# Output stage of a gated SSM and MLP mixer: other load order, five skip slots, a snapshot home of its own, and a reordered last group

## The chip, the cores and the metric

The kernel runs on one core of one Trainium2 chip. The metric is the device time of one execution in microseconds (us); the median of several executions is compared. A core has a matrix engine (TensorE, PE in the profile), a vector engine (VectorE, DVE), a scalar engine (ScalarE, ACT), GpSimd (POOL) and SyncE (SP). In this kernel SP issues most loads, ACT issues the stores of the output, and POOL issues the transfers that add to what is at their destination. PE writes its sums into eight PSUM banks of 128 x 512 fp32.

## The reference, cut to what matters

The input x has 2048 rows (time) of 1024. Two branches are computed from it and mixed with a gate per row:

```python
x = A_x
g = sigmoid((x * gate_w).sum(-1, keepdims=True))
Lam = Lambda_re + 1j * Lambda_im
dt = exp(log_dt); Lam_bar = exp(dt * Lam)
Bu = x @ (((Lam_bar - 1) / Lam)[:, None] * Bmat).T
h[t] = Lam_bar * h[t - 1] + Bu[t]                    # over 2048 steps
a = 2 * real(h @ Cmat.T) + x * Dskip
y = layernorm(x)
b = gelu(y @ w1 + b1) @ w2 + b2                      # 1024 -> 3584 -> 1024
out = g * a + (1 - g) * b
```

## The kernel before, in words

The program is a graph of tasks. Each task names its engine, a planned duration, a priority, the buffers that it reads and writes, and the function that emits the instruction. A planner (`schedule`) plays the graph through with the planned durations (`c_mm`, `c_act`, `c_dve`, `c_scan`, a model of the DMA queues) and fixes an order on each engine and queue; each engine then runs its list strictly in that order, and waits on semaphores where a task depends on another engine. So a changed duration in the planner can move instructions anywhere, though it changes no dependency. The order on PE is pinned: each product depends on the one before (`pe_last`).

The stages on PE, with the profile's times:

- Up to 130 us: transposes and B x (L825), results stored to DRAM as `scr_u`.
- 130 to 475 us: the MLP, in two halves of the hidden width and two halves of the rows: blocks "m" (x w1, gelu) and "b" (times w2). Partial sums of "b" go to DRAM (`scr_ac`) by POOL, the second half with an accumulating store (L1243). Beside it, DVE runs the recurrence (L970, L973, scans L984); the states go to DRAM as `scr_h`.
- From 475 us: the output stage "y", states times C, eight groups y0 to y7 of two row tiles of 128 each. Row tiles are used in the order 8 to 15, then 0 to 7 (`YORD`).

Every group in "m", "b" and "y" is a 2 x 2 block product done with seven products in place of eight (class `SG`, L1029 and, where a bank is begun, L1027). A product in "y" is 8 matmuls of 128 x 128 by 128 x 512. Each group has three PSUM banks: `a`, `e` and `b`. Its products: p1 fills `a`, and ACT copies `a` to `b` (`seed`, L1053); p5 fills `e`, ACT snapshots it (`s5`, L1045); p6 adds to `b`, ACT snapshots it (`su`, L1045); p2 completes `a`, p3 completes `e`, p7 adds to `b` (one result is taken there) and p4 adds to `b` (the last result). The pinned order from group to group is: p1 of the next group, p7 of the one before, p5, p6, p2, p3, then p4 of the one before. The last group ends with p7 and p4, one right behind the other.

What the output stage adds up for row tile k is, in the names of the tasks:

- `bb` (ACT, L1308): (1 - g) b2 into a summand buffer `AV` (eight of 128 x 1024 fp32).
- `acl` (POOL queue, L1310): the MLP's partial sums from `scr_ac`, added to it by the transfer.
- `yx` (SP queue, L1311): the tile of x into a skip buffer `XV`; `xd` (DVE, L1312): times Dskip, in place; `xa` (DVE, L1313): times g, added to the summand.
- `oa` (DVE, L1332) adds g times a snapshot to half of the summand, and `o` (DVE, L1334) adds g times a PSUM bank and writes 512 columns of the output tile; when both halves are there, `out` (ACT queue, L1339) stores 128 x 1024.
- `hg` (SP queue, L1298): the states of a group, 1 MB; `ys` (DVE, L1081): four sums and differences of them, weights of p5, p6, p7 and p3.

`y_load(yi)` records `hg`, `bb`, `acl`, `yx`, `xd`, `xa` of a group, `y_prep` the `ys`, `y_group` the rest. Where a load is recorded decides which earlier readers of its buffer it must wait for. `y_load` of groups 0 and 1 is recorded in the last "b" group, of 2 and 3 at the first y group, and of x + 3 in group x after p4 of group x - 1. From group 4 on, `hg` also waits for the last product recorded so far. The skip buffers: tiles 0 to 3 in order of use (row tiles 8 to 11) share `XV[0]`, the later ones alternate between two others. `XV[0]` is also the home of the snapshot `su` of even groups (`YU[0]`).

Of the kernel before, what the change touches and what calls it, by code (L numbers as in the profile page):

```python
# [45 lines left out]


def c_scan(N):
    return 0.12 + N / 480.0


class Buf:
# [367 lines left out]
def build(nc, A_x, A_Lambda_re, A_Lambda_im, A_B_re, A_B_im, A_C_re, A_C_im, A_log_dt, A_Dskip,  # L420
          B_x, B_w1, B_b1, B_w2, B_b2, gate_w, out, stats=None):
    x2 = A_x[0]
    out2 = out[0]
# [20 lines left out]
    g = Graph()  # L444
    es = ExitStack()
    with es:
# [30 lines left out]
        HT = AR.alloc(28672)  # L477
# [5 lines left out]
        SSM = AR.alloc(20480)  # L483
# [38 lines left out]
        def ssem(name, k, final=False):  # L522
            key = (name, k)
            if key not in slot_sems:
                slot_sems[key] = sem("d_%s%d" % (name, k), dram=final)
                if final:
                    final_sems.append(slot_sems[key])
            return slot_sems[key]
# [60 lines left out]
        def bcast(ap, off, name):  # L589
# [11 lines left out]
              reads=[b_ones], writes=[b_ident], name="ident")  # L601
# [167 lines left out]
        for k in range(LT):  # L769
            n = 1 << k  # L770
# [478 lines left out]
        H0 = [SSM, SSM + 8192] + [HT + 8192 * i for i in range(4)] + [SSM, SSM + 8192]  # L1249
        YR = HT + 49152  # L1250
        AV = [TABR + 4096 * i for i in range(4)] + [YR + 4096 * i for i in range(4)]
        XV = [SSM + 16384, YR + 16384, YR + 18432]
        DB = SSM + 18432
        OV = [YR + 20480 + 2048 * i for i in range(4)]
        YS = [SQ + 7168, HT + 32768]
        YU = [SSM + 16384, HT + 40960]
        CQ = {"B11": 0, "B21": 1, "B22": 2, "T1": 3, "T2": 4, "T3": 5, "T4": 6, "B12": 6}
        YORD = (4, 5, 6, 7, 0, 1, 2, 3)

# [34 lines left out]
        def y_load(yi):  # L1294

            qb = YORD[yi]
            o = AR.v(H0[yi], [(1, 2 * UE)])
            g.dma((52.0, yi), lambda e: e.dma_start(out=o.ap, in_=HS[qb]), 2 * UE * 128 * 2, ssem("hg", yi), reads=[b_hs[pg][qb] for pg in range(PG)], writes=[o], name="hg%d" % yi,  # L1298
                  extra=pe_last if yi > 3 else ())
            if yi == 0:  # L1300
                g.dma((51.0, 0), lambda e: e.dma_start(out=v_db.ap, in_=bass.AP(A_Dskip.tensor, A_Dskip.offset, [[0, 128], [1, D]])), 128 * D * 2, sem("d_dskb"), writes=[v_db], name="dskb")
            for t in range(2):
                n = 2 * yi + t
                k = 2 * qb + t
                av = AR.v(AV[n % 8], [(1, D)], F32)
                xi = 0 if n < 4 else 1 + n % 2
                xv = AR.v(XV[xi], [(1, D)])
                g.add("act", c_act(D, psum=False, ap_operands=1), (52.0, n), lambda e, av=av, k=k: e.activation(av.ap, v_b2.ap, AF.Copy, scale=C("GM1", k)),  # L1308
                      reads=[v_b2, bc("GM1")], writes=[av], name="bb%d" % k)
                g.dma((52.0, n), lambda e, av=av, k=k: e.dma_start(out=av.ap, in_=ACS[k], accum_op=ALU.add), 128 * D * 4, ssem("yac", n % 8), reads=[b_acs[k], av], writes=[av], name="acl%d" % k, q="pool").slack = 1.0  # L1310
                g.dma((52.0, n), lambda e, xv=xv, k=k: e.dma_start(out=xv.ap, in_=x2[k * 128:(k + 1) * 128, :]), 128 * D * 2, ssem("yx", xi), writes=[xv], name="yx%d" % k)  # L1311
                g.add("dve", c_tt16(D), (52.0, n), lambda e, xv=xv: e.tensor_tensor(xv.ap, xv.ap, v_db.ap, ALU.mult), reads=[xv, v_db], writes=[xv], name="xd%d" % k)  # L1312
                g.add("dve", c_dve(D), (52.0, n, 1), lambda e, xv=xv, av=av, k=k: e.scalar_tensor_tensor(av.ap, xv.ap, C("G", k), av.ap, ALU.mult, ALU.add),  # L1313
                      reads=[xv, av, bc("G")], writes=[av], name="xa%d" % k)

        def y_group(yi):
            qb = YORD[yi]
            st = {"A11": [hk(yi, 0, 0, k) for k in range(PT)], "A12": [hk(yi, 1, 0, k) for k in range(PT)], "A22": [hk(yi, 1, 1, k) for k in range(PT)]}
            for i in range(4):
                st["S%d" % (i + 1)] = [ysq(yi, i, k) for k in range(PT)]  # L1320
            mv = {nm: [cq(nm, k) for k in range(PT)] for nm in ("B11", "B21", "B22", "T1", "T2", "T3", "T4")}
            su, s5 = AR.v(YU[yi % 2], [(1, 512)], F32), AR.v(AO + 16384, [(1, 512)], F32)
            done = {}

            def fin(qd, q, bk):
                t, dh = qd // 2, qd % 2
                n, k = 2 * yi + t, 2 * qb + t
                a = AR.v(AV[n % 8] + dh * 2048, [(1, 512)], F32)
                o = AR.v(OV[n % 4] + dh * 1024, [(1, 512)])
                if dh == 1:  # L1330
                    sv = su if t == 0 else s5
                    g.add("dve", c_dve(512), (10.0, q - 2), lambda e: e.scalar_tensor_tensor(a.ap, sv.ap, C("G", k), a.ap, ALU.mult, ALU.add),  # L1332
                          reads=[sv, a, bc("G")], writes=[a], name="oa%d" % k)
                g.add("dve", c_dve(512), (10.0, q), lambda e: e.scalar_tensor_tensor(o.ap, V(PS[bk], 0, [(1, 512)]), C("G", k), a.ap, ALU.mult, ALU.add),  # L1334
                      reads=[b_ps[bk], a, bc("G")], writes=[o, b_ps[bk]], name="o%d.%d" % (k, dh))
                done[qd] = True
                if done.get(2 * t) and done.get(2 * t + 1):
                    ov = AR.v(OV[n % 4], [(1, D)])
                    g.dma((10.0, q + 2), lambda e: e.dma_start(out=out2[k * 128:(k + 1) * 128, :], in_=ov.ap), 128 * D * 2, ssem("out", n % 4, True), reads=[ov], name="out%d" % k, q="act")  # L1339
            return SG("_y%d" % yi, st, mv, fin, su, s5)  # L1340
# [42 lines left out]
        for n, it in enumerate(flat):  # L1383
            bi, x = it
            kind, Fh, c = blocks[bi]
            last_of_block = (n + 1 == len(flat)) or flat[n + 1][0] != bi
            nit = None if n + 1 == len(flat) else flat[n + 1]
            if (kind, Fh, c, x) == ("b", 1, 0, 3):
                y_load(0)
                y_load(1)  # L1390
            if (kind, x) == ("y", 0):
                for yi in range(2, 4):
                    y_load(yi)
            if cur is None:
                cur = make(it)
                cur.p1()

            if prev is not None:
                prev.p7()
            if kind == "b" and x + 1 < 4:  # L1400
                prep_s((bi, x + 1), seq[0] + 4)
            if kind == "b" and Fh == 1 and c == 0 and x == 3:
                y_prep(0, seq[0] + 4)
            if kind == "y":
                if x + 1 < 8:
                    y_prep(x + 1, seq[0] + 4)
            if not early5:
                cur.p5()
            early5 = False
            cur.p6()  # L1410
            cur.p2()
            cur.p3()
            if prev is not None:
                prev.p4()
                if kind == "y" and 1 <= x and x + 3 < 8:
                    y_load(x + 3)
                if kind == "m" and x > 0:
                    w1_next(18)
            prev, cur = cur, pend
            pend = None  # L1420
            if last_of_block:
                if nit is None:
                    prev.p7()
                    prev.p4()
                else:
                    nk = blocks[nit[0]][0]
                    if nk == "b":
                        prep = True
                        b0 = None

                        cur = make(nit)
                        prev.p7()
                        cur.p1()
                        prev.p4()
                        w1_next(20)
                        prep_s(nit, seq[0])
                        pend = make((nit[0], nit[1] + 1))
                        pend.p1()
                    else:
                        cur = make(nit)  # L1440
                        prev.p7()
                        cur.p1()
                        cur.p5()
                        early5 = True
                        prev.p4()
                    prev = None
                if (kind, Fh, c) == ("m", 1, 0):
                    ct_load(seq[0] + 20)

                if kind == "m":  # L1450
                    if (Fh, c) == (0, 0):
                        xn_load(1, seq[0] + 20)
                    elif (Fh, c) == (1, 1):
                        xn_load(0, seq[0] + 20)
                elif (Fh, c) == (0, 1):
                    w2_load(1, seq[0] + 30)
# [43 lines left out]
```

## Time and profile before

| what | us |
|---|---|
| median of 7 runs | 579.3 (577.74 to 583.58) |
| the profiled execution | 583.58 |
| its span | 581.8 |
| PE busy in the span | 558.1 |
| DVE busy in the span | 479.8 |
| output stage, from p1 of y0 to the end of the span | 474.8 to 581.8 |
| load of a skip tile, issue to landing (16 of them): shortest, median, longest | 2.6, 7.4, 11.2 |
| load of a group's states, issue to landing (8): shortest, median, longest | 6.0, 7.1, 11.5 |

The profile is of one execution, the slowest of the seven. PE's busy time is nearly the span, so the time is made where PE waits; the busy times of the other engines matter only through those waits. A wait is named after what came last, and that may itself have been held up by what stands ahead of it in its engine's or queue's list. Task names like `yx11` carry the row tile, `hg3`, `seed_y1` the group; they follow from the order of the instructions of a line on its engine.

### The profile page before, as it was taken

The numbers are of one execution on the slowest core, as the hardware profiler recorded it, in microseconds if no ns is written. First come the engines' busy times: TensorE is split into PE (matmuls) and PEld (weight loads), VectorE is DVE, ScalarE is ACT, GpSimd is POOL, SyncE is SP. The second block draws the span as 40 slices with busy tenths as digits, with TensorE's granted clock in tenths as the row PEclk, the third lists the DMA queues.
The fourth block names the chain that finished last, engine by engine and source line by source line (L and its number), as shares of the span: only waits on it lengthen the run. The fifth ranks groups of instructions, "written<-read, shape, count | busy, mean of one in ns | idle before, by whom it ended". The sixth has DMA issues, their size and how long they took to land.

```text
span 581.8 us, 7338 instructions
## 1 busy us (share of the span) xinstructions
PE 558.1 (96%) x2608; PEld 255.2 (44%) x2657; DVE 479.8 (82%) x817; ACT 271.1 (47%) x433; POOL 76.5 (13%) x110
## 2 busy tenths in 40 slices
PE   4999999997999999999999999999999999799997
PEld 3544444443444444444444444444444444344442
DVE  2799719949999999999999999999346785779843
ACT  2844871345674335864326673336863352222210
POOL 0070144000000111001120000130100231111000
PEclk9999999999999999999999999999999999999999
DMA  8999848999399733648379699987999599799601
GB/s 249 252 265 378 320 118 255 298 287 381 123 345 231 254 145 152 257 163 293 159 262 353 197 279 264 208 158 196 291 292 198 90 235 267 203 276 270 210 37 55
DMA packets 124543, 134.76 MB, mean 232 GB/s; under 512 B 70482, under 2 KB 100178, under 8 KB 123482
## 3 DMA queue, kind: packets, MB, share of 16 engines
q1 hardware_dynamic: 99664, 70.81, 43.6%
q0 software_dynamic: 11232, 46.40, 28.9%
q10 hardware_dynamic: 13610, 17.08, 8.6%
q8 instruction: 21, 0.34, 0.3%
q14 instruction: 16, 0.13, 0.1%
HBM read 63.74 MB, written 54.80 MB: 204 GB/s over the span
## 4 chain that ended last, share of the span: by engine, by line
PE 66%; DVE 16%; DMA 9%; issue 6%; ACT 1%; POOL 1%; SPq 1%; ACTq 0%; DVEq 0%; POOLq 0%
PE ps L1029 39%; PE ps L1027 14%; PE ps L825 11%; DVE ar L1081 4%; DMA ar<-scr_ac 3%; DVE ar L970 3%; DVE ar L984 3%; DMA ar<-in_A_x_dram 3%; DVE ar L973 2%; DMA ar<-in_B_w_dram 2%; DVE ar L1163 2%; DMA scr_ac<-ar 2%; DVE ar L871 1%; POOL scr_ac L1243 1%; PE ps L666 1%
## 5 line engine op out<-in xcount | busy, mean ns | idle before, releaser
L1029 PE MATMUL ps<-ar 128*128 128x512 f16 (+1 forms) x1419 | 327.1, 380 | 9.5 <-ACT ps L1053 4.0
L1029 PEld LDWEIGHTS ps<-ar 128*128 128x128 f16 (+1 forms) x1440 | 140.7, 98 | 180.6 <-ACT ps L1053 5.1
L1027 PE MATMUL ps<-ar 128*128 128x512 f16 (+1 forms) x560 | 137.5, 379 | 2.0 <-DVE ar L1081 1.2
L1081 DVE TENSOR_TENSOR ar<-ar 128x896 f16<-128x896 bf16 (+8 forms) x176 | 118.2, 707 | 18.4 <-DMA ar<-scr_xn 7.6
L825 PE MATMUL ps<-ar 128*128 128x512 bf16 x500 | 111.6, 382 | 0.9 <-issue 0.4
L984 DVE TENSOR_TENSOR_SCAN ar<-cst,init,ar 128x256 bf16<-128x256 f32 x128 | 86.9, 732 | 0.3
L1027 PEld LDWEIGHTS ps<-ar 128*128 128x128 bf16 (+1 forms) x576 | 56.1, 98 | 70.5 <-DVE ar L1081 3.1
L970 DVE TENSOR_TENSOR ar<-ar 128x2048 bf16<-128x2048 bf16 x64 | 77.0, 1217 | 2.8 <-DMA ar<-scr_u 2.8
L825 PEld LDWEIGHTS ps<-ar 128*128 128x128 bf16 x512 | 50.0, 99 | 60.6 <-issue 2.1
L832 ACT ACTIVATE ar<-ps 128x512 bf16<-128x512 f32 x64 | 37.0, 595 | 49.5 <-PE ps L825 27.9
L1045 ACT ACTIVATE ar<-ps 128x512 f32<-128x512 f32 x72 | 42.2, 592 | 36.3 <-PE ps L1027 26.3
L1053 ACT ACTIVATE ps<-ps 128x512 f32<-128x512 f32 x52 | 30.3, 582 | 40.4 <-PE ps L1027 32.6
L1159 ACT ACTIVATE ar<-ps,cst 128x512 bf16<-128x512 f32 x56 | 38.4, 685 | 20.7 <-PE ps L1029 20.1
L1163 DVE TENSOR_TENSOR ar<-ps,ar 128x512 f32<-128x512 f32 x56 | 38.0, 679 | 11.3 <-PE ps L1029 11.0
L1046 ACT ACTIVATE ar<-ps,cst 128x512 f32<-128x512 f32 x32 | 22.0, 687 | 52.9 <-PE ps L1027 33.2
L1165 ACT ACTIVATE ar<-ar,cst 128x512 bf16<-128x512 f32 x56 | 40.1, 716 | 13.0 <-DVE ar L1163 12.9
L973 DVE TENSOR_TENSOR ar<-ar 128x1024 bf16<-128x1024 bf16 x64 | 42.0, 684 | 0.3
L1231 ACT ACTIVATE ar<-ps,cst 128x512 f32<-128x512 f32 x32 | 22.0, 687 | 42.5 <-PE ps L1029 42.5
L1334 DVE SCALAR_TENSOR_TENSOR ar<-ps,cst,ar 128x512 bf16<-128x512 f32 x32 | 23.9, 748 | 12.4 <-PE ps L1029 12.4
L1308 ACT ACTIVATE ar<-ar,cst 128x1024 f32<-128x1024 bf16 x16 | 18.3, 1146 | 28.5 <-DVE ar L1334 27.1
L1234 DVE SCALAR_TENSOR_TENSOR ar<-ps,cst,ar 128x512 f32<-128x512 f32 x32 | 23.7, 740 | 7.4 <-PE ps L1029 6.6
L1310 POOL DMA_DIRECT2D ar<-scr_ac x16 | 14.0, 878 | 89.9 <-ACT ar L1308 58.3
(98 smaller groups left out, 228.0 us busy)
## 6 DMA issues: line engine op xcount, KB each, us to landing
scr_ac<-ar POOLq DMA_DIRECT2D x32, 512.0 KB, 7.0
scr_w<-ar POOLq DMA_DIRECT2D x14, 896.0 KB, 5.7
ar<-scr_w SPq DMA_DIRECT2D x14, 896.0 KB, 6.1
ar<-in_A_x_dram SPq DMA_DIRECT2D x32, 256.0 KB, 7.1
scr_u<-ar ACTq DMA_DIRECT2D x32, 256.0 KB, 5.9
ar<-scr_u SPq DMA_DIRECT2D x16, 512.0 KB, 7.7
scr_h<-ar POOLq DMA_DIRECT2D x16, 512.0 KB, 6.0
ar<-scr_ac POOLq DMA_DIRECT2D x16, 512.0 KB, 9.5
```

Of the source, the lines that this page charges most:

```text
L825: ins = e.matmul(V(PS[bk], 0, [(1, CH)]), ws[dt].ap, xs[dt].ap, start=(dt == 0), stop=(dt == DT - 1))
L832: g.add("act", c_act(CH), pr, lambda e, ev=ev, bk=bk: e.activation(ev.ap, V(PS[bk], 0, [(T, 2), (1, T)]), AF.Copy), reads=[b_ps[bk]], writ ...
L970: g.add("dve", c_tt16(UE), pri(i), lambda e: e.tensor_tensor(o.ap, a.ap, tbl.ap, ALU.mult), reads=[a, tbl], writes=[o], name=nm + tag)
L973: g.add("dve", c_tt16(UE // 2), pri(i), lambda e: e.tensor_tensor(o.ap, a.ap, b.ap, op), reads=[a, b], writes=[o], name=nm + tag)
L984: lambda e, pt=pt, ri=ri, vin=vin, go=go: e.tensor_tensor_scan(go.ap, Cb("R", pt, T), vin.ap, V(INIT, pt * 2 + ri, [(1, 1)]), ALU.mult, AL ...
L1027: ins = e.matmul(V(PS[bk], 0, [(1, n)]), st[i].ap, mv[i].ap, start=(i == 0), stop=(i == K - 1))
L1029: ins = e.matmul(V(PS[bk], 0, [(1, n)]), st[i].ap, mv[i].ap, start=False, stop=(i == K - 1), skip_group_check=True)
L1045: return e.activation(o.ap, V(PS[bk], 0, [(1, 512)]), AF.Copy)
L1081: g.add("dve", c_tt16(n), (10.0, q), lambda e: e.tensor_tensor(o.ap, a.ap, b.ap, op), reads=[a, b], writes=[o], name=nm).slack = slack
L1159: g.add("act", c_act(512, ap_operands=1), (10.0, q + 1), lambda e: e.activation(o.ap, V(PS[bk], 0, [(1, 512)]), AF.Gelu_apprx_tanh, bias=C ...
L1163: g.add("dve", c_dve(512), (10.0, q - 2), lambda e: e.tensor_tensor(sv.ap, V(PS[bk], 0, [(1, 512)]), sv.ap, ALU.add), reads=[b_ps[bk], sv] ...
L1165: g.add("act", c_act(512, psum=False, ap_operands=1), (10.0, q + 3), lambda e: e.activation(o.ap, sv.ap, AF.Gelu_apprx_tanh, bias=C("B1", ...
```

## The change

Six edits, all but the first in the output stage:

- the planned duration of a scan is longer (0.719 us in place of 0.653 for 256 columns);
- two more skip buffers, so that tiles from the fifth on go through four in place of two;
- the snapshot `su` of even groups gets memory of its own in place of `XV[0]`;
- `y_load` of group 3 is no longer recorded at the first group, and that of later groups one group later than before: two groups ahead in place of three; `hg` waits for the last recorded product from group 3 on;
- in the last group p7 comes before p3 in place of after p4 of the group before;
- the last group's output is stored in halves of 512 columns, each when it is ready.

```diff
 def c_scan(N):
-    return 0.12 + N / 480.0
+    return 0.15 + N / 450.0
...
-        XV = [SSM + 16384, YR + 16384, YR + 18432]
+        XV = [SSM + 16384, YR + 16384, YR + 18432, HT + 43008, HT + 45056]
...
-        YU = [SSM + 16384, HT + 40960]
+        YU = [HT + 47104, HT + 40960]
...
-                  extra=pe_last if yi > 3 else ())
+                  extra=pe_last if yi > 2 else ())
...
-                xi = 0 if n < 4 else 1 + n % 2
+                xi = 0 if n < 4 else 1 + n % 4
...
-                if done.get(2 * t) and done.get(2 * t + 1):
+                if yi == 7:
+                    g.dma((10.0, q + 2), lambda e: e.dma_start(out=out2[k * 128:(k + 1) * 128, dh * 512:(dh + 1) * 512], in_=o.ap), 128 * 1024, ssem("outl", qd, True), reads=[o], name="out%d.%d" % (k, dh), q="act")
+                elif done.get(2 * t) and done.get(2 * t + 1):
...
             if (kind, x) == ("y", 0):
-                for yi in range(2, 4):
-                    y_load(yi)
+                y_load(2)
...
             cur.p6()
             cur.p2()
+            if nit is None:
+                cur.p7()
             cur.p3()
             if prev is not None:
                 prev.p4()
-                if kind == "y" and 1 <= x and x + 3 < 8:
-                    y_load(x + 3)
+                if kind == "y" and 1 <= x and x + 2 < 8:
+                    y_load(x + 2)
...
                 if nit is None:
-                    prev.p7()
                     prev.p4()
```

## The prediction

> **What bounds the kernel now.** I read the page's busy line first, then what TensorE (PE) waits for, then the timeline around those waits, then the DMA queues in the same stretch.
>
> ```profile
> PE 558.1 (96%) x2608; PEld 255.2 (44%) x2657; DVE 479.8 (82%) x817; ACT 271.1 (47%) x433; POOL 76.5 (13%) x110
> ```
>
> PE is the bound: 558.1 of 581.8 us, and back-to-back matmuls of 512 columns start 216 ns apart. No matmul is added or removed, so the change can only touch PE's idle time. The waits of PE (total us, times, longest):
>
> ```profile
> PE ps L650 <- DMA ar<-in_A_x_dram: 7.7, 2, 5.8
> PE ps L1029 <- ACT ps L1053: 4.0, 1, 4.0
> PE ps L1029 <- ACT ar L1045: 3.0, 1, 3.0
> PE ps L1027 <- DVE ar L1081: 1.2, 3, 0.5
> PE ps L1029 <- DVE ar L1334: 0.9, 1, 0.9
> ```
>
> 7.7 us is the start, out of reach. 4.0 and 0.9 lie in the output stage, 3.0 in the first MLP group, 1.2 at three starts of a second-GEMM block. So about 5 us (0.9%) is the most that the edits of the output stage can win. The timeline where the output stage begins (start, length, engine, line; in brackets the idle time before and who ended it):
>
> ```profile
> 486.31 0.69 DVE L1312 TENSOR_TENSOR ar<-ar 128x1024 bf16<-128x1024 bf16 x1 [2.06 <-DMA ar<-in_A_x_dram]
> ...
> 488.31 0.74 DVE L1334 SCALAR_TENSOR_TENSOR ar<-ps,cst,ar 128x512 bf16<-128x512 f32 x1
> ...
> 489.08 0.36 ACTq L1339 DMA_DIRECT2D out_dram<-ar  x1
> 489.54 0.58 ACT L1053 ACTIVATE ps<-ps 128x512 f32<-128x512 f32 x1 [7.50 <-DVE ar L1334]
> 490.04 1.14 ACT L1308 ACTIVATE ar<-ar,cst 128x1024 f32<-128x1024 bf16 x1
> ...
> 490.18 7.08 PE L1029 MATMUL ps<-ar 128*128 128x512 f16 x32
> ...
> 500.54 0.69 DVE L1312 TENSOR_TENSOR ar<-ar 128x1024 bf16<-128x1024 bf16 x1 [2.35 <-DMA ar<-in_A_x_dram]
> ...
> 505.82 0.58 ACT L1053 ACTIVATE ps<-ps 128x512 f32<-128x512 f32 x1
> ...
> 506.45 7.08 PE L1029 MATMUL ps<-ar 128*128 128x512 f16 x32 [4.01 <-ACT ps L1053]
> ```
>
> One chain appears twice. A skip row tile (256 KB of x) lands late; DVE's `xd` (L1312) waits for it; the output sum `o` (L1334) is queued behind on DVE; ACT's store of that output waits for `o`; ACT's `seed` (L1053) is queued behind the store; PE's p6 needs the seed. It costs 0.3 us at p6 of group y1 (PE was free at 489.9, started 490.18) and 4.2 us at p6 of y2 (502.3 to 506.45). So what counts is when each skip tile lands, and what stands ahead of each seed. In this stretch two queues share the DMA engines; the DMA view of 478.4 to 485:
>
> ```profile
> q0 software_dynamic: 288, 1.05, 79.7%
> q1 hardware_dynamic: 291, 0.58, 26.2%
> ```
>
> Equal packet counts, 44 per us each. The two skip tiles loaded there (`yx12`, `yx13`) are about 144 packets each, so one takes 3.3 us while POOL's 512 KB accumulating transfers (q0) are pending.
>
> The tail: PE waits 0.91 us for DVE to empty a PSUM bank before the last product, and the last sum follows.
>
> ```profile
> 575.80 0.75 DVE L1334 SCALAR_TENSOR_TENSOR ar<-ps,cst,ar 128x512 bf16<-128x512 f32 x1 [1.04 <-PE ps L1029]
> ...
> 576.61 1.90 PE L1029 MATMUL ps<-ar 128*128 128x512 f16 x8 [0.91 <-DVE ar L1334]
> ...
> 578.55 0.75 DVE L1334 SCALAR_TENSOR_TENSOR ar<-ps,cst,ar 128x512 bf16<-128x512 f32 x1 [2.00 <-PE ps L1029]
> ```
>
> [...] after the 3.0 us wait, the 8 matmuls from 142.41 took 3.46 us instead of 1.73. After the 4.0 us wait it did not drop (506.45: 32 matmuls in 7.08 us).
>
> **The change part by part.**
>
> *Skip tiles.* Before, tiles 8 to 11 (in order of use) share one slot: each load waits for the `xa` of the tile before. `yx12` to `yx15` go through two slots, so `yx15` and `yx14` cannot be issued until `xa13` and `xa12` are done (488.42, 493.17). After, four slots serve tiles from 12 on. In the built order SP issues, behind one another, `yx14`, `yx15` (when p3 of the last second-GEMM group is done, near 471.7), `yx12`, `yx13` (474.75, as now), then `yx11`. That last one matters. In the kernel before it was issued at 449.41 and landed at 452.00, because DVE did `xd10`, `xa10` early. In the built order after, `yx10` comes behind the four C transposes and `xd10`, `xa10` stand behind `ac1.3.1` and `ys4_1`. Those two take place at 471.7 to 473.1; 0.69 + 1.28 us more put `xa10` at 475.0, and `yx11` is issued about 475.6, fifth in the queue.
> Landing: under this load the first packet of `yx15` came 3.6 us after its issue (488.42 to 492.02); so the five start near 475.3, and 5 x 144 / 44 = 16.4 us later, at 491.7, the fifth is through; semaphores came 0.5 to 1.3 us after last packets. **`yx11` lands near 492.6.** POOL's loads hold their times: they lose about 1 us to the two early tiles and win it back because `hg3` (1 MB, 479.76 to 491.22) has moved to after p4 of y0. Hence `acl12` (491.84) is not late.
>
> *First wait.* DVE after: ..., `xd12`, `xd11`, `o8.1`, .... `xd11` 492.6, `o8.1` ends 492.6 + 0.65 + 0.75 = 494.0. ACT after: store, then `bb0` (L1308), then the seed of y1, where before the seed came first. From end of `o8.1` to p6 took 1.13 us (489.05 to 490.18); `bb0` adds its pitch of 1.03. p6 of y1 starts 496.2: a wait of 6.3 us instead of 0.3. Queued behind on DVE: `xa11`, `xa12`, `o9.1` (done 497.9; p4 of y0 needs it at 501.4: no wait).
>
> *Second wait.* From 496.2, p6 of y2 is due seven products of 1.73 us later, 508.3. DVE after `o9.1` (497.9) has nine operations up to `o10.1`: `xa15` and `xa13` of 1.28 and seven of about 0.65, so 505.0. Store, `bb2`, seed as above: 507.2. So this 4.2 us wait goes, with 1 us to spare. Sum of both: 6.3 - 0.3 - 4.2 = **+1.8 us**.
>
> *Later groups.* An `hg` load is now issued one group (12.1 us) before its p1 instead of two; the median landing is 7.1 us, the longest 11.5, and the prep `ys` needs another 2.5 us but p5 comes 3.5 us after p1. I take 0; if cover is gone, up to 2 us once. `bb`, `acl` keep their POOL places. The snapshot's own home frees `su` of y0 from `xa11`: su of y0 was not waited for (481.45), so 0; without this edit it would now wait for `xa11`.
>
> *Clock.* [...] 0 to 2.5 us, I take **+0.8**.
>
> *Tail.* p7 of y7 moves ahead of p3, so two products (3.4 us) lie between it and p4: -0.9. Its `su` has p2's 1.73 us to be made in, against 0.6. Four half stores replace two stores: two more issues of 0.34 us on ACT, idle there. The last store moves 128 KB: DVE's last sum ended 579.30, the span 581.8; a 256 KB store ran its packets in 0.83 us, so -0.2 (0 to -0.4). **-1.1.**
>
> *Planner cost.* A scan was planned at 0.653 us, now at 0.719; measured 0.732. This reorders DVE from 100 us on. First MLP group: `cadd0.0.1` moves behind two more scans (2 x 0.66): the 3.0 us wait, s5 behind that gelu, grows 1.3; DVE is full there from 131 to 180, later `cadd`s are up to 1.9 late against 0.6 us of room before a seed: +0.9 (0 to 2.5). Starts of second-GEMM blocks: the first gets 0.84 us more work ahead of its `hs1`, part of that same lateness; the second and third (waits of 0.25 and 0.54) get 0.6 and 2.6 us less SSM work ahead: -0.8. **+0.1.**
>
> Sum: 1.8 + 0.8 - 1.1 + 0.1 = **+1.6 us**. The profiled execution took 583.58 (span 581.8), the median is 579.3: the profiled one is the slowest of the seven, so some of its waits may be smaller elsewhere. 583.6 would become 585.2; on the median I say **580.9**.
>
> **Rivals.** *A: `yx11` is no bottleneck, 0.22.* If skip tiles get through faster than 44 packets per us (an uncongested one landed in 2.6 us), `xd12` sets `o8.1` at 488, p6 of y1 waits 0.5, and the y2 wait goes: -4.0 - 1.1 and 0.1: 574.3; if it lands at 489, half: 577. For: the runs without profile are shorter. Against: the packet counts.
> *B: the clock decides, 0.18, slower.* [...] 2.5 us instead of 0.8, 1.8 + 2.5 - 1.1 + 0.1 = +3.3, 582.6. It decides once the clock is at half for over 4.2 us (a loss of 2.1). For: the drop after 139 us. Against: the 4.0 us wait left the clock alone.
> *C: DVE's new order costs the first MLP group its whole bound, 0.15, slower.* 2.5 instead of 0.9: 1.8 + 0.8 - 1.1 + 1.7 = +3.2, 582.5. For: DVE has no gap there from 131 to 180, and seeds have 0.6 us of room. Against: each `cadd` that is late in one group leaves less ahead of the next.
> *D: the change doesn't do what it says.* Neither wait depends on the slots, as it would be if skip tiles were held by the transfers alone; then only the tail is won, -1.1, 578.2. It lies in the main case (0.45, its own range 577.5 to 582.2).
>
> **Numbers.** Half a percent is 2.9 us, about what a measurement of this kernel can tell from no change. Faster by that needs A: 0.22. Slower needs B or C, or both (585): 0.33. The main case and D make up 0.45. The range, 575.4 to 585.0, goes from a little above A's full gain to B and C together.
>
> **What would show it.** Right: PE's wait for L1053 moves from 502 to about 490 and is near 6 us, `xd11` (L1312) waiting for a skip tile near 492; no wait before the last product; the waits of L1027 for L1081 down to one. Wrong: L1053 gone from PE's waits (A), or the granted clock at half after 496 for over 3 us (B).

## The result, and the profile after

The changed kernel takes 586.71 us (median of 15 runs, 582.65 to 591.57), the kernel before, beside it, 580.08 (36 runs). Ratio 1.0107, 95% interval 1.008 to 1.0134: **slower by 6.2 us (4.6 to 7.8)**, outside the predicted range (575.4 to 585.0). All ratios here leave out runs more than 1.5% above the fastest of their kernel; medians are over all runs, so the two can differ a little.

The profiled execution took 587.56 us, span 585.5. Busy times, then PE's waits (total us, times, longest):

```profile
PE 558.8 (95%) x2607; PEld 256.0 (44%) x2657; DVE 481.3 (82%) x817; ACT 270.7 (46%) x433; POOL 74.1 (13%) x110
```

```profile
PE ps L1029 <- ACT ps L1053: 7.0, 2, 6.8
PE ps L650 <- DMA ar<-in_A_x_dram: 6.6, 2, 5.6
PE ps L1029 <- ACT ar L1045: 5.7, 1, 5.7
PE ps L1027 <- DVE ar L1081: 1.2, 3, 0.6
```

PE's work is the same (558.8 against 558.1). The wait for L1334 is gone: the tail edit did what it says. The seed's wait (L1053) is still one long wait, 6.8 us instead of 4.0. The wait for a snapshot (L1045) in the first MLP group went from 3.0 to 5.7.

The timelines of DVE, ACT and PE where the output stage begins (start, length, engine, line; in brackets the idle time before it and who ended it):

```profile
487.36 0.69 DVE L1312 TENSOR_TENSOR ar<-ar 128x1024 bf16<-128x1024 bf16 x1
493.76 0.69 DVE L1312 TENSOR_TENSOR ar<-ar 128x1024 bf16<-128x1024 bf16 x1 [5.71 <-DMA ar<-in_A_x_dram]
494.37 0.74 DVE L1334 SCALAR_TENSOR_TENSOR ar<-ps,cst,ar 128x512 bf16<-128x512 f32 x1
```

```profile
495.15 0.36 ACTq L1341 DMA_DIRECT2D out_dram<-ar  x1
495.55 1.15 ACT L1308 ACTIVATE ar<-ar,cst 128x1024 f32<-128x1024 bf16 x1 [13.08 <-DVE ar L1334]
496.61 0.58 ACT L1053 ACTIVATE ps<-ps 128x512 f32<-128x512 f32 x1
```

```profile
497.24 9.23 PE L1029 MATMUL ps<-ar 128*128 128x512 f16 x32 [6.77 <-ACT ps L1053]
...
511.49 3.83 PE L1029 MATMUL ps<-ar 128*128 128x512 f16 x17
```

This is the predicted chain, link by link. `yx11`, issued at 476.08 as the fifth skip load, landed at 493.74; `xd11` (the second L1312) waited 5.71 us for it; `o8.1` (L1334) stood behind; then the store, `bb0` (L1308), the seed (L1053), and p6 of y1 at 497.24 after 6.77 us of idle PE. p6 of y2 (511.49) has no wait. What the prediction had too small stands in the length of the first PE row: 9.23 us for 32 matmuls that take 7.08 at full clock. The table of the windows around it (stretch, its length, busy times; the sixth value after the comma, PEclk, is the granted clock):

```profile
490.00:494.80 4.80, 0.47 (x3) 0.00 (x0) 1.04 (x2) 0.00 (x0) 0.00 (x0) 1.00 1.06 245
494.80:501.60 6.80, 4.36 (x11) 1.61 (x12) 6.80 (x9) 2.75 (x4) 0.85 (x1) 0.50 0.77 163
501.60:508.00 6.40, 6.35 (x30) 2.88 (x30) 6.30 (x9) 1.15 (x1) 0.29 (x1) 1.00 0.61 181
```

The clock is at half for 6.8 us, from 2.4 us before PE came back until 4.4 us after: 9.23 - 7.08 = 2.15 us lost.

The first MLP group of the changed kernel, on PE (here too the clock was at half for 6.8 us, from 139.8 to 146.7; 8 matmuls take 1.90 us at full clock, as in e11's row below):

```profile
143.19 3.59 PE L1029 MATMUL ps<-ar 128*128 128x512 bf16 x8 [5.70 <-ACT ar L1045]
```

And the tail, the last products of PE without a gap, then DVE's last sum:

```profile
571.92 10.52 PE L1029 MATMUL ps<-ar 128*128 128x512 f16 x47
```

```profile
582.49 0.75 DVE L1334 SCALAR_TENSOR_TENSOR ar<-ps,cst,ar 128x512 bf16<-128x512 f32 x1 [0.97 <-PE ps L1029]
```

### The profile page after: what moved, and what is told of

Same layout as the page of the kernel before. It is cut to its first block, busy times and chain, and to the rows that moved or that the text cites. A ratio compares the mean times of both kernels' runs of the same rounds, so it can differ in the third digit from the quotient of the medians.

```text
span 585.5 us, 7342 instructions
## 1 busy us (share of the span) xinstructions
PE 558.8 (95%) x2607; PEld 256.0 (44%) x2657; DVE 481.3 (82%) x817; ACT 270.7 (46%) x433; POOL 74.1 (13%) x110
## 4 chain that ended last, share of the span: by engine, by line
PE 78%; DVE 12%; DMA 6%; issue 2%; SPq 1%; ACT 1%; ACTq 0%; DVEq 0%
PE ps L1029 48%; PE ps L1027 18%; PE ps L825 11%; DMA ar<-in_A_x_dram 4%; DVE ar L984 3%; DVE ar L970 3%; DMA ar<-in_B_w_dram 2%; DVE ar L973 2%; DVE ar L1081 2%; DVE ar L871 1%; DVE ar L1163 1%; PE ps L666 1%; SPq L957 0%; PE ps L891 0%; DVE ar L1334 0%
## 5 line engine op out<-in xcount | busy, mean ns | idle before, releaser
L1027 PE MATMUL ps<-ar 128*128 128x512 f16 (+1 forms) x560 | 137.5, 379 | 1.9 <-DVE ar L1081 1.2
L1081 DVE TENSOR_TENSOR ar<-ar 128x896 f16<-128x896 bf16 (+8 forms) x176 | 117.2, 708 | 18.4 <-DMA ar<-scr_xn 5.8
L825 PE MATMUL ps<-ar 128*128 128x512 bf16 x500 | 110.6, 380 | 0.9 <-issue 0.4
L1027 PEld LDWEIGHTS ps<-ar 128*128 128x128 bf16 (+1 forms) x576 | 56.2, 98 | 70.4 <-DVE ar L1081 3.1
L825 PEld LDWEIGHTS ps<-ar 128*128 128x128 bf16 x512 | 49.9, 98 | 59.8 <-issue 1.0
L1045 ACT ACTIVATE ar<-ps 128x512 f32<-128x512 f32 x72 | 42.2, 592 | 39.7 <-PE ps L1027 27.3
L832 ACT ACTIVATE ar<-ps 128x512 bf16<-128x512 f32 x64 | 36.9, 595 | 48.8 <-PE ps L825 26.5
L1163 DVE TENSOR_TENSOR ar<-ps,ar 128x512 f32<-128x512 f32 x56 | 38.2, 682 | 14.0 <-PE ps L1029 12.1
L1053 ACT ACTIVATE ps<-ps 128x512 f32<-128x512 f32 x52 | 30.3, 583 | 36.0 <-PE ps L1027 34.8
L1308 ACT ACTIVATE ar<-ar,cst 128x1024 f32<-128x1024 bf16 x16 | 18.2, 1145 | 34.2 <-DVE ar L1334 32.4
L1334 DVE SCALAR_TENSOR_TENSOR ar<-ps,cst,ar 128x512 bf16<-128x512 f32 x32 | 23.9, 747 | 11.3 <-PE ps L1029 11.0
```

Source lines behind the costliest of these rows:

```text
L825: ins = e.matmul(V(PS[bk], 0, [(1, CH)]), ws[dt].ap, xs[dt].ap, start=(dt == 0), stop=(dt == DT - 1))
L832: g.add("act", c_act(CH), pr, lambda e, ev=ev, bk=bk: e.activation(ev.ap, V(PS[bk], 0, [(T, 2), (1, T)]), AF.Copy), reads=[b_ps[bk]], writ ...
L1027: ins = e.matmul(V(PS[bk], 0, [(1, n)]), st[i].ap, mv[i].ap, start=(i == 0), stop=(i == K - 1))
L1045: return e.activation(o.ap, V(PS[bk], 0, [(1, 512)]), AF.Copy)
L1081: g.add("dve", c_tt16(n), (10.0, q), lambda e: e.tensor_tensor(o.ap, a.ap, b.ap, op), reads=[a, b], writes=[o], name=nm).slack = slack
L1163: g.add("dve", c_dve(512), (10.0, q - 2), lambda e: e.tensor_tensor(sv.ap, V(PS[bk], 0, [(1, 512)]), sv.ap, ALU.add), reads=[b_ps[bk], sv] ...
```

## The experiments

The theory with which I began them: the buffers and the tail bring little, and the *planned scan cost* loses the time, in two places: the order around block 11 in the output stage (late `xd10`, late `yx11`, a long wait, two windows of half clock), and the order ahead of the output stage. Rivals: the output stage's order alone, the front alone, or the edits of loads and buffers themselves.

All kernels of the study, with the edit of each. "Half-clock windows" is worked out from each run's mean granted clock: (1 - clock) x span x 2 / 3.41 us, averaged over the runs. A window here is 3.41 us: the clock stood at half for 3.41 us in the trace of before and twice for 6.83 us in that of the changed kernel. One costs at most 1.7 us of matmul time, if PE is busy in all of it (in e0, 32 matmuls behind a wait took 8.76 us in place of 7.08).

| kernel | scan cost | median us (runs) | ratio to before (95%) | half-clock windows per run |
|---|---|---|---|---|
| before | old | 579.5 to 581.1 | 1 | 1.7 to 1.9 |
| changed | new | 586.71 (15) | 1.0107 (1.008 to 1.0134) | 3.1 |
| e1: scan cost alone | new | 588.43 (4) | 1.0142 (1.0089 to 1.0195) | 3.1 |
| e2: all but the scan cost | old | 579.72 (14) | 0.997 (0.9936 to 1.0005) | 1.5 |
| e3: last group alone | old | 579.63 (22) | 0.9995 (0.9971 to 1.002) | 1.6 |
| e4: changed, first skip products early | new | 587.12 (6) | 1.0105 (1.0061 to 1.015) | 2.9 |
| e5: new for units 0 to 4 | mixed | 582.97 (22) | 1.0031 (1.0007 to 1.0055) | 1.8 |
| e6: new from unit 5 on | mixed | 582.39 (22) | 1.0061 (1.004 to 1.0082) | 2.6 |
| e7: e2, blocks 12 to 15 later | old | 573.18 (6) | 0.9887 (0.9839 to 0.9935) | 0.7 |
| e8: e2, block 8's product late | old | 582.11 (14) | 1.0024 (0.9998 to 1.005) | 2.5 |
| e9: e4 and e7's edit | new | 579.69 (22) | 0.9963 (0.9937 to 0.999) | 1.2 |
| e10: new for units 5 to 11 | mixed | 578.65 (22) | 0.997 (0.9946 to 0.9994) | 1.2 |
| e11: e9, old for unit 0 | mixed | 575.48 (21) | 0.9931 (0.9905 to 0.9957) | 0.4 |
| e14: new for units 12 to 15 | mixed | 578.06 (22) | 0.9975 (0.9951 to 1.0) | 1.2 |
| e15: new for unit 0 | mixed | 585.66 (20) | 1.0063 (1.0031 to 1.0095) | 2.7 |

A unit is one SSM step of DVE, 8 scans (four channel groups, real and imaginary part); two halves of the channels by eight blocks of 256 rows make 16 units. e12 and e13 gave no time; e14 and e15 are the same two kernels. Differences between two kernels below are differences of ratios times 580 us; their half-widths are the root of the summed squares.

### The kernel before once more

> The kernel before, unchanged, for a second profile. The change moved the median by 6.6 us but the two profiled executions by only 4.0. Theory X (the first profile of before is of a slow execution): here one of its waits is smaller, the 3.0 us one before the first MLP group with its half clock, or the 4.2 us one at p6 of y2, and the span is near 578. Theory Y (the waits of before are fixed): both waits come again within 0.5 us.

One execution, 576.8 us. PE's waits:

```profile
PE ps L650 <- DMA ar<-in_A_x_dram: 5.7, 1, 5.7
PE ps L1029 <- ACT ps L1053: 4.0, 1, 4.0
PE ps L1027 <- DVE ar L1081: 1.4, 3, 0.6
PE ps L1029 <- DVE ar L1334: 0.9, 1, 0.9
```

The 3.0 us wait for L1045 isn't there. The profile from which I predicted had caught the kernel before with a wait in its first MLP group that this execution doesn't have. The waits of the output stage are the same to a tenth.

### The scan cost alone, all but it, and the tail alone

e1 is the kernel before with the first hunk of the diff. e2 is the changed kernel without it:

```diff
 def c_scan(N):
-    return 0.15 + N / 450.0
+    return 0.12 + N / 480.0
```

e3 is the kernel before with the last group's order and half stores only.

> The kernel before with nothing but the longer planned scan (0.15 + N / 450). In its built order xd10 and xa10 stand behind ac1.3.1, so yx11 is issued near 475.6, third behind yx12 and yx13, and lands near 490; su of y0 still shares the slot of that tile, so it waits for xa11 (near 494.5), and p7 of y0 (due 486.4) for it. Theory S (the planned scan cost makes the loss, by the place of xd10): PE waits about 8 us at p7 of y0, slower than before by 4 to 8 us. Theory L (the new slots and load order make the loss, the scan cost does not): within 1.5 us of before. Theory M (the loss is in the first MLP group): slower by about 1 to 3 us, with the wait of 3.0 us near 139 grown to 4 to 6 and no long wait at 486.

> The changed kernel with the old planned scan (0.12 + N / 480), all edits of the output stage kept. xd10, xa10, xd11, xa11 stand early on DVE again and yx11 is issued at 449; but o8.1 now stands behind xd12 and xd13, and yx13 is fourth of four skip tiles issued from 471.7: 4 x 144 packets at 44 per us from 475.3 end at 488.4, landing near 489.3. o8.1 ends near 491.3, seed of y1 behind out8 and bb0, p6 of y1 near 493.5: a wait of 3.6 us in place of 0.3, the wait of 4.2 us at y2 gone, 1.1 us won at the end. Theory S: -1.5 us against before, give or take 1.5, so at least 4 us faster than the changed kernel. Theory L: as slow as the changed kernel, +5 to +7. Theory M: -1 to -4.

> The kernel before with only the last group's new product order and the half stores. All theories: the wait of 0.9 us before the last product goes, and the last store is shorter; -1.1 us (-0.9 to -1.3), a ratio of 0.998. If the half stores or two more issues cost anything, nearer to -0.7.

The planned cost of a scan, which computes nothing, is the cause: alone it loses 8.2 us (1.0142), and without it the changed kernel is level with the kernel before. Where PE idles longest in the output stage: the line of e1's waits (it lies at p7 of y0, 484 to 492 us, since `su` of y0 has to wait for `xa11` in the old home of the snapshot), then PE's rows of e2 and e3:

```profile
PE ps L1029 <- ACT ar L1045: 7.4, 1, 7.4
```

```profile
493.17 8.77 PE L1029 MATMUL ps<-ar 128*128 128x512 f16 x32 [3.89 <-ACT ps L1053]
```

```profile
499.89 5.49 PE L1029 MATMUL ps<-ar 128*128 128x512 f16 x18 [4.05 <-ACT ps L1053]
```

e3 keeps the wait of the kernel before (at p6 of y2) and loses only the 0.9 before the last product; its time does not change measurably (-0.3 us, -1.7 to +1.2). In e2 the wait at y2 is gone and one of the same size stands at p6 of y1. DVE's rows of e2 say why the new buffers did not remove it:

```profile
486.50 0.69 DVE L1312 TENSOR_TENSOR ar<-ar 128x1024 bf16<-128x1024 bf16 x1 [0.50 <-DMA ar<-in_A_x_dram]
489.70 0.69 DVE L1312 TENSOR_TENSOR ar<-ar 128x1024 bf16<-128x1024 bf16 x1 [2.51 <-DMA ar<-in_A_x_dram]
490.31 0.74 DVE L1334 SCALAR_TENSOR_TENSOR ar<-ps,cst,ar 128x512 bf16<-128x512 f32 x1
```

`o8.1`, ready to go, stands behind `xd12` and `xd13`, whose tiles are four and five places further on in the output and still in the DMA queue. In the kernel before `o8.1` stood behind the same two products, but there `yx12` and `yx13` were the first two of these loads (issued from 474.75). The new buffers let `yx14` and `yx15` be issued ahead of them (from 470.97 in e2), so that `yx13` is the fourth: `xd13` begins at 489.70 in place of 486.31.

### Splitting the scan cost by place

```diff
# e4
-                g.add("dve", c_tt16(D), (52.0, n), lambda e, xv=xv: e.tensor_tensor(xv.ap, xv.ap, v_db.ap, ALU.mult), reads=[xv, v_db], writes=[xv], name="xd%d" % k)
-                g.add("dve", c_dve(D), (52.0, n, 1), lambda e, xv=xv, av=av, k=k: e.scalar_tensor_tensor(av.ap, xv.ap, C("G", k), av.ap, ALU.mult, ALU.add),
+                g.add("dve", c_tt16(D), ((9.0, n) if n < 4 else (52.0, n)), lambda e, xv=xv: e.tensor_tensor(xv.ap, xv.ap, v_db.ap, ALU.mult), reads=[xv, v_db], writes=[xv], name="xd%d" % k)
+                g.add("dve", c_dve(D), ((9.0, n, 1) if n < 4 else (52.0, n, 1)), lambda e, xv=xv, av=av, k=k: e.scalar_tensor_tensor(av.ap, xv.ap, C("G", k), av.ap, ALU.mult, ALU.add),
# e5
-                    g.add("dve", c_scan(T), pri(10 + ri * 4 + a),
+                    g.add("dve", c_scan(T) if un < 5 else 0.12 + T / 480.0, pri(10 + ri * 4 + a),
# e6
-                    g.add("dve", c_scan(T), pri(10 + ri * 4 + a),
+                    g.add("dve", 0.12 + T / 480.0 if un < 5 else c_scan(T), pri(10 + ri * 4 + a),
```

> The changed kernel with one edit: the scaled products of the first four skip blocks (xd and xa, n under 4) get priority 9.0 instead of 52.0. VectorE then does xd10, xa10, xd11, xa11 ahead of the last scan's products, as with the old scan cost, and block 11's load is issued right after block 10's; the front part is the changed kernel's own. Theory Y (half of the loss is the order around block 11, half is the front part): the 6.8 us wait on L1053 falls to about 3.9 at the first output slice, as in the all-but-scan kernel, with one window of half clock instead of two; the time is 583.3 us, 3 to 4 below the changed kernel. Theory O (the order around block 11 alone): 579.7. Theory F (the front part alone, the first MLP group's wait of 5.7 us on L1045): 586.7, no change.

> The changed kernel with the new scan cost for the first five SSM units only, the old one after that. VectorE's order is that of the changed kernel in the front part, and that of the all-but-scan kernel at the output stage. Theory Y: 583.3 us, the wait on L1045 ahead of the first MLP group at 5 to 6 us and the one on L1053 at about 3.9 us. Theory O: 579.7. Theory F: 586.7.

> The changed kernel with the old scan cost for the first five SSM units and the new one after that: VectorE's order is that of the kernel before in the front part, and that of the changed kernel at the output stage (block 11's load fifth in its queue, xd11 late, o8.1 behind it). Theory Y: 583.3 us, no wait of over 3 us ahead of the first MLP group, and 6.8 us on L1053 at the first output slice with two windows of half clock. Theory O: 586.7. Theory F: 579.7.

The medians of e5 and e6 fell where both places count (582.97 and 582.39 for 583.3). The two share out all units between them: e5 is 3.5 us (half-width 2.4) above e2 and e6 5.3 (2.3), together 8.8, and the changed kernel is 7.9 (2.5) above e2. e5 idles 3.5 us at p6 of y1, e6 7.0 us with two windows of half clock (mean clock 0.994 over 579.8 us). The wait of 5 to 6 us at L1045 that was expected of e5 is not in its trace; PE idles 3.1 us earlier there, at L825 for ACT's L832. e4's trace did what was expected in the output stage,

```profile
492.12 8.77 PE L1029 MATMUL ps<-ar 128*128 128x512 f16 x32 [4.24 <-ACT ps L1053]
```

but its time was 587.12, not 583.3: a miss that a theory of two additive places does not explain (taken up below). The trace is of the fastest of its six executions (581.67 us), so it does not show what the others lost.

### The order around block 11 by itself

e8 is e2 with one task placed later by the planner, `xd8` (n = 0 is row tile 8; `xd9` and `xd10` follow through the slot that they share), and holds the changed kernel's order from `xd9` on:

```diff
-                g.add("dve", c_tt16(D), (52.0, n), lambda e, xv=xv: e.tensor_tensor(xv.ap, xv.ap, v_db.ap, ALU.mult), reads=[xv, v_db], writes=[xv], name="xd%d" % k)
+                g.add("dve", c_tt16(D), (52.0, n), lambda e, xv=xv: e.tensor_tensor(xv.ap, xv.ap, v_db.ap, ALU.mult), reads=[xv, v_db], writes=[xv], name="xd%d" % k).slack = 8.0 if n == 0 else 0.0
```

> The all-but-scan kernel (old scan cost everywhere) with the scaled product of block 10 alone placed 8 us later in the planner's order. From block 8's product on, every queue then holds the changed kernel's order (block 11's load fifth among the skip loads, xd12, xd11 and then o8.1 on VectorE), while everything up to the third MLP block keeps the old order. If the order around block 11 costs by itself what the traces show (from the start of the wait on L1053 to the end 95.4 and 95.6 us in the changed kernel and with the old front, 92.0 and 92.4 with the early order): a wait of 6.8 us on L1053 with two windows of half clock, and 579.7 + 3.4 = 583.1 us. Rival: the whole loss sits ahead of the output stage, as the early-skip-products kernel's time of 587.1 suggests: 579.7, no change from the all-but-scan kernel.

Two rows of its trace, DVE and PE:

```profile
483.40 0.69 DVE L1312 TENSOR_TENSOR ar<-ar 128x1024 bf16<-128x1024 bf16 x1 [5.70 <-DMA ar<-in_A_x_dram]
```

```profile
486.88 8.53 PE L1029 MATMUL ps<-ar 128*128 128x512 f16 x32 [6.13 <-ACT ps L1053]
```

The long wait, the two windows (mean clock 0.994 over 574.4 us) and +3.1 us against e2 (0.6 to 5.6; expected 3.4) come with this order alone. The traces agree: from the start of y0's seed (ACT, L1053) to the end of the span it is 107.2 to 108.7 us with the late order (e8, e6, the changed kernel), and 103.1 to 105.5 where the other edits of the output stage stand with the early one (e2, e4, e5, e10, e14, e15). e4 has 105.5 there and the changed kernel 108.5: in the output stage e4's edit did bring its 3 us.

### Taking the queue in front of `o8.1` away

e7 is e2 with the same kind of edit on other tasks, `.slack = 12.0 if 4 <= n < 8 else 0.0`: the products of blocks 12 to 15 no longer stand ahead of `o8.1`.

> The all-but-scan kernel (old scan cost everywhere) with the scaled products of blocks 12 to 15 placed up to 12 us later in the planner's order, so that o8.1 on VectorE is no longer queued behind products that wait for their loads. If o8.1 behind those waits is what holds the first output slice, o8.1 ends near 486 instead of 491, the 3.9 us wait on L1053 goes or falls under 1 us, with no half clock there, and the time is about 575.5, 3 to 5 below both kernels. Rival: the wait comes back a slice later, since o9.0 is now queued behind xd12 and xa12, which wait for the load of acl12 at about 491.8: a wait of 2 to 4 us on L1053 at p6 of y2, and the time stays at 579 to 580.

DVE and PE:

```profile
485.53 0.75 DVE L1334 SCALAR_TENSOR_TENSOR ar<-ps,cst,ar 128x512 bf16<-128x512 f32 x1 [0.98 <-PE ps L1029]
```

```profile
490.51 7.07 PE L1029 MATMUL ps<-ar 128*128 128x512 f16 x32
...
502.59 2.75 PE L1029 MATMUL ps<-ar 128*128 128x512 f16 x12
```

`o8.1` now waits for PE's result only, no seed is waited for at y1 (490.51) or y2 (502.59), and the rival (the wait returns at y2) is refuted. 573.18 us, ratio 0.9887: faster than both kernels, 4.8 us below e2 (1.4 to 8.2). Up to `o8.1` the loads are issued in the order of e2 (behind `yx2`, `hg3` and `hg4` come earlier); what differs ahead of this sum is DVE's list. From the start of y0's seed to the end it is 99.4 to 99.7 us in the traces of e7, e9 and e11, in place of e2's 105.2.

### Which units lose the time ahead of the output stage

e9 has the new cost everywhere, e4's early products and e7's edit; e11 is e9 with the old cost for unit 0. e10, e14 and e15 are e2 with the new cost for a few units (in the manner of e5's line: `5 <= un < 12`, `un >= 12`, `un < 1`).

> The changed kernel with its new scan cost kept everywhere, and two edits at the output stage: the first four skip products at priority 9.0 (early), those of blocks 12 to 15 placed up to 12 us later. VectorE's order at the output stage is that of the later-skip-sums kernel, the rest is the changed kernel's. No wait of over 1 us on L1053 is expected. If the new scan cost loses 3.6 us ahead of the output stage and 3.4 there: 573.2 + 3.6 = 576.8 us. Rival, all of the 7 us lost ahead of the output stage: 580.2.

> The changed kernel with the new scan cost for SSM units 5 to 11 alone, the old one before and after; the output stage keeps the early order. If the first five units (up to about the first MLP group) carry what is lost ahead of the output stage: 579.7 us, the time of the all-but-scan kernel. Rival, the middle units carry about 4 us of it (early-skip-products 587.1 less new-front-old-order 583.0): 583.7, with waits between the first second-GEMM group and the output stage longer than before.

> The kernel with the new scan cost and no wait in the output stage (579.7 us), with the old scan cost for SSM unit 0 alone. VectorE then does nb0.0 ahead of the table scales G and GM1, for which it waits until about 81 to 84 us, instead of behind them (1.3 us of work moves into that idle time), and the sum cadd0.0.1 of the first MLP group comes behind two scans instead of four (1.3 us earlier). If these two moves carry what is lost ahead of the output stage: from the end of VectorE's wait on L932 to fx3_0.2 32.8 us instead of 34.0, no wait of over 3 us on L1045 after 135 us, and 576 us, 3.7 lower. Rival: the loss sits in the later order of the first five units, and the time stays at 579.7; if the two moves count but once, without the clock that a wait costs, 578.3.

> The all-but-scan kernel with the new scan cost for SSM units 12 to 15 alone; the output stage keeps the early order. If the first five units and the late order at block 11 carry the whole loss: 579.7 us, a ratio of 0.997 to the kernel before. Rival: the last units carry what two pairs of runs leave over (0.4 to 0.7%): 582 to 584 us.

> The all-but-scan kernel with the new scan cost for SSM unit 0 alone: nb0.0 goes behind G and GM1, and cadd0.0.1 behind five scans instead of two; the output stage keeps the early order. If unit 0's two moves carry what the first five units cost: a wait of 3 us or more on L1045 near 136 to 140 us, fx3_0.2 34 us after G instead of 32.8, and 583.2 us, a ratio of 1.003. Rival: the order of units 1 to 4 carries it: 579.7 us, a ratio of 0.997.

Against e2, the new cost for units 5 to 11 changes nothing measurable (0.0, half-width 2.4), for units 12 to 15 nothing (+0.3, 2.5); for units 0 to 4 it costs 3.5 (2.4), and for **unit 0 alone 5.4 us (2.7)**; the last two are not apart by the noise. In the other direction, e11 against e9 is -1.9 (2.2) by the ratios and -4.2 by the medians: the same sign, not clear by itself. What unit 0's cost moves first is seen on DVE, in the changed kernel and then in e11. First around 70 to 85 us:

```profile
70.22 1.22 DVE L970 TENSOR_TENSOR ar<-ar 128x2048 bf16<-128x2048 bf16 x1
82.72 0.22 DVE L934 TENSOR_SCALAR cst<-cst 128x16 f32<-128x16 f32 x1 [11.28 <-ACT cst L932]
...
83.00 1.21 DVE L970 TENSOR_TENSOR ar<-ar 128x2048 bf16<-128x2048 bf16 x1
```

```profile
70.07 1.22 DVE L970 TENSOR_TENSOR ar<-ar 128x2048 bf16<-128x2048 bf16 x1
...
71.29 1.22 DVE L970 TENSOR_TENSOR ar<-ar 128x2048 bf16<-128x2048 bf16 x1
83.71 0.20 DVE L934 TENSOR_SCALAR cst<-cst 128x16 f32<-128x16 f32 x1 [11.21 <-ACT cst L932]
```

DVE waits 11 us for the gate (L932). The second product, `nb0.0`, was done ahead of that wait and is now done after it: 1.2 us of work taken out of idle time and put behind it. Then the first sum of the MLP, `cadd0.0.1` (L1163), again the changed kernel and e11:

```profile
138.63 2.68 DVE L984 TENSOR_TENSOR_SCAN ar<-cst,init,ar 128x256 bf16<-128x256 f32 x4
141.23 0.67 DVE L1163 TENSOR_TENSOR ar<-ps,ar 128x512 f32<-128x512 f32 x1
```

```profile
136.17 1.39 DVE L984 TENSOR_TENSOR_SCAN ar<-cst,init,ar 128x256 bf16<-128x256 f32 x2
137.48 0.67 DVE L1163 TENSOR_TENSOR ar<-ps,ar 128x512 f32<-128x512 f32 x1
```

Four scans ahead of it instead of two: 1.3 us more. PE's row of e11 to be held against the changed kernel's 5.70 us at 143.19, and that of e15:

```profile
139.50 1.90 PE L1029 MATMUL ps<-ar 128*128 128x512 bf16 x8 [0.69 <-ACT ar L1045]
```

```profile
146.11 3.52 PE L1029 MATMUL ps<-ar 128*128 128x512 bf16 x8 [3.08 <-ACT ar L1045]
```

3.52 us for 8 matmuls in e15, against 1.90 in e11, is half clock again. e15's output stage takes as long as e2's (104.8 and 105.2 us from the seed of y0), so its loss lies ahead of it. The other traces point the same way. From 60 to 160 us PE waits for other engines 3.6 to 8.1 us in each of the six with the new cost for unit 0 (e1, e4, e5, e9, e15, the changed kernel); of the ten with the old one, seven wait 1.2 us at most, and three (before, e2, e7) 3.0 to 5.2. Not all of it lies in the first MLP group: e1 and e5 have no wait at L1045 there, and idle 3.3 and 3.1 us at L825 instead, as e2 and e7 do.

e15, with e11 of the same sign, shows that unit 0's planned cost by itself costs about what is lost ahead of the output stage. By which of its moves is not shown. Every kernel with the new cost for unit 0 has the two above, and they are not all: the traces of e2 and e15 have another operation (by line or shape) in 298 of the 817 places of DVE's list, from 70 to 473 us.

### What stays open

Two pairs leave more than these parts: e6 against e8 (2.1, half-width 1.9) and e4 against e5 (4.3, 2.9), in which the new cost from unit 5 on is added. e10 and e14 show nothing for those units one set at a time, so either it takes both sets, or e4 (6 runs) is off. Also open is what makes the stretch from 115 to 145 us differ so much between executions of one order: in the traces with the old cost for unit 0, DVE's waits for the normalized rows (`scr_xn`) come to 1.4 us in one and 10.1 in another. The averages above rest on many runs for that reason.

## Why the prediction was wrong, step by step

| step | predicted us | measured us |
|---|---|---|
| `yx11` lands | 492.6 | 493.74 |
| wait at p6 of y1 in place of that at y2 | +1.8 | +2.3 in the trace (6.77 - 0.3 - 4.2) |
| clock in the output stage | +0.8 (0 to 2.5) | +2.15 in the trace |
| `hg` one group ahead, the snapshot's own home | 0; without the home a wait for `xa11` | no wait of either kind in the trace; e1, without the home, waits 7.4 for `xa11` |
| tail | -1.1 | -0.9 and -0.24 in the trace; e3's time -0.3 (-1.7 to +1.2) |
| planner's cost ahead of the output stage | +0.1 | +3.5 (2.4) for units 0 to 4 in e5, +5.4 (2.7) for unit 0 in e15 |

(The second part of the tail: from the end of the last sum to the end of the span 2.50 us before, 585.5 - 583.24 = 2.26 after.)

**Right: the mechanism in the output stage.** The two equal packet rates (44 per us each: 288 and 291 packets in 6.6 us before, 619 and 618 in 14 us after), the fifth place of `yx11` and the order of DVE's list behind `xd11` gave the place of the wait and its length within 0.5 us (in part by luck: `yx11` landed 1.1 us later than predicted, and PE was free 0.6 us later). e8 shows that this order costs its time by itself, e7 that with the new buffers in place the wait goes once `o8.1` no longer stands behind the products. What the prediction did not ask is what the new buffers do without the late `yx11`: e2 shows that they move the wait of y2 to y1 and no more, because `o8.1` comes behind `xd12` and `xd13`, whose loads now come behind `yx14` and `yx15`.

**Too small: the clock.** I took +0.8 out of 0 to 2.5, and gave rival B, with its 2.5, a 0.18; how long the clock would stay at half was my estimate in both, not shown by the trace of before. I held against B that the trace of before showed no drop after its 4.0 us wait. B held in the changed kernel: its sign was a clock at half for over 4.2 us, and it was 6.8. Over all runs the changed kernel has 1.2 to 1.4 half-clock windows more than the kernel before, at 1.7 us at most 2.0 to 2.4 of the 6.2 us, shared by both places. The two traces say the same: 3.9 us lost at half clock in the changed kernel (2.15 and 1.7), 1.6 in the kernel before. The single observation was not typical: the same wait of 4.0 us was followed by a half-clock window in e0 (32 matmuls in 8.76 us) and e3 (8.51 us).

**Wrong: the planner's cost.** This step failed in three ways. It said that the new cost "reorders DVE from 100 us on"; the reorder begins at 70 us, and the move of `nb0.0` out of the idle time before L934 was not in the sum at all. It put the first MLP group at +0.9, at most 2.5; for everything ahead of the output stage the runs give 3.5 and 5.4. Rival C, DVE's new order at the cost of the first MLP group, fits the traces of the changed kernel and of e15, with a bound that was too low (by the prediction's own terms B and C together make 584.2 us, not 585); in e1 and e5 the idle time lies ahead of that group. And it credited -0.8 at the starts of the second-GEMM blocks; those waits (L1027 for L1081) are 1.2 us in both traces. The profile helped it to go wrong: with a wait of 3.0 us in that group already there, a later `cadd0.0.1` looked like a small addition; e0, and e3 with the same order there, don't have that wait. That such executions have more to lose is likely, but not shown.

The parts add up within their noise: e2 against before -1.7, the order around block 11 +3.1, units 0 to 4 +3.5 make +4.9 us (half-width 2.9); with unit 0's value from e15 (5.4) it is +6.8 (3.1). Measured: +6.2 (4.6 to 7.8).

## What to carry to other kernels

Where a planner fixes the order of strict queues, a better estimate of one duration is an edit of every queue: compare the whole order before and after, from the first instruction that moves, and look for work that leaves an idle stretch and for critical sums that get something with a late load in front of them. Before adding buffers against a wait, look at what stands ahead of the waiting engine's needed operation in its queue; here moving the products of four tiles behind it (e7) won 1.1%, while the new buffers (e2) moved the wait to another place, since they also let later loads go ahead of earlier ones. A wait of PE of 3 to 4.6 us counted for more than its length in most of these traces (in e0, 4.03 us of wait and then 1.7 us lost at half clock), and a profile of one execution is to be read beside others before its waits are taken as the kernel's.

## What the runs showed of the hardware that was not expected

Within the span the granted clock stood at half for 3.41 us in the trace of before, and twice for 6.83 us, two such windows, in that of the changed kernel. The mean clocks of the other traces, to three digits, come near whole numbers of windows too: 0.997 is one, 0.994 two (e6, e8), 0.991 three (e2, e15), 0.988 four (e1); e3's 0.996 comes to 1.3. How many followed a wait depended on its length only roughly. In the output stage, waits of 3.8 to 4.2 us were followed by one window in e0, e2, e3, e4, e10 and e15 (the third of e15's trace; the others come behind waits that ended at 119.43 and 146.11), by none in the profile of before (32 matmuls in 7.08 us); 3.5 us by none in e5 (28 matmuls in 6.22 us); 6.1 to 7.0 us by two in e6, e8 and the changed kernel; 7.4 us by three in e1 (of its four, one lies ahead of the output stage, where 52 matmuls from 119.01 took 13.14 us). Why equal waits had unequal effects is not shown.

Waits shorter than 3.41 us were followed by a drop as well: 3.0 us (before, 8 matmuls in 3.46 us) and 3.1 us (e15, 3.52 us) in the first MLP group; 2.9 us in that group of e4 was not (1.90 us). Two windows after 6.1 us were only in rival B; three after 7.4 us were in no estimate.
